# Two decode layers on one core: how the weights change places between the first layer and the second

## The chip, the cores and the metric

The kernel runs on one core of a Trainium2 chip. The metric is the device time of one execution in microseconds (us). Everything is f32. The inputs lie in HBM, and SyncE's DMA queue brings them into SBUF; the other engines compute from there.

## The reference

Two layers are computed, each an attention over a cache and then a GELU block, with the same weights and the same caches both times:

```python
x = A_x
x = x + _A_ref(_layernorm(x), A_k_cache, A_v_cache, A_wq, A_wo)
x = x + _B_ref(_layernorm(x), B_w1, B_b1, B_w2, B_b2)
x = x + _A_ref(_layernorm(x), A_k_cache, A_v_cache, A_wq, A_wo)
x = x + _B_ref(_layernorm(x), B_w1, B_b1, B_w2, B_b2)
# _A_ref: q = x @ wq (32 heads of 128), scores against k (4 key heads, 4096 long),
#         softmax, p @ v, then @ wo
# _B_ref: gelu(x @ w1 + b1) @ w2 + b2
```

There are B = 8 sequences with one token each, D = 1024, F = 3584. wq and wo have 16 MiB each, w1 and w2 14 MiB each, and k and v 64 MiB each. Read twice each, that is 376 MiB; what stays in SBUF between the layers needn't be read again.

## The kernel before

SBUF holds an `arena` of 52 units. A unit is 1024 columns of 128 partitions, 512 KiB. Every transfer goes through a list written out by hand, `stream`: each entry has a key, a number of units, its source and the units at which it may begin. `pump` (L207) issues entries from the head of the list as long as their units are free; `release` (L219) frees a used slot and calls `pump`. SyncE thus issues the DMAs in the list's order, each when the last readers of its units have ended, and nothing overtakes. Units 48 to 51 (`OWN`) are the kernel's own, for the softmax rows and their transposes.

For a sequence b, `attention` (L434) goes through eight pieces of K, each 1 MiB (`scores`, L341: 4 matmuls of 512 columns), then `probs` and `turn` (maximum, exponential, transposes), then eight pieces of V (`values`, L393), with `heads` after each pair. Layer 0 goes through the sequences 0 to 7, layer 1 through 7 to 0, so that the K of sequence 7 is kept. In layer 0 the caches pass through units 16 to 47, 16 units (8 MiB) at a time. Units 0 to 15 hold half of wq throughout; a further part of wq is parked in PSUM (`spot`) and in `spare`.

`expand` (L233) multiplies the normalized rows xnT with wq or w1; `project` (L317) multiplies with wo or w2. After wo and after w2, `layernorm` (L178) needs the whole row x before anything of wq or w1 can begin. At the turn of the layers the program ends w2, norms x and then goes through wq: half of it is resident, seven transfers bring the rest. 15 of the 28 row tiles of w2 stay for layer 1 (7.5 MiB), all eight pieces of sequence 7's K too. In layer 1 the 13 other tiles of w2 come last; the tiles that were kept are multiplied while w1's second half arrives (`begin`, L555). `add_b2` (L323) adds the bias by matmuls into the same sums.

A matmul of the program stands as two instructions in the profile.

Of the kernel before, what the change touches and what calls it, by code (L numbers as in the profile page):

```python
# [8 lines left out]
F32 = mybir.dt.float32  # L9
# [27 lines left out]
OWN = 48  # L37
RING = 32
R_AT = (48, 50)
CACHE_AT = (16, 48), (0, 32)  # L40
CUTS = {(0, "k", B - 1): (4, 2, 2), (0, "v", B - 1): (2, 2, 2, 2), (1, "v", B - 1): (4, 4), (1, "k", B - 2): (4, 4), (1, "v", 0): (4, 4)}
# [6 lines left out]
class Arena:  # L48


    def __init__(self, ap):
        self.ap = ap
        self.freed = dict.fromkeys(range(N_UNIT), 0)
        self.clock = 0
        self.limit = OWN

# [9 lines left out]
    def own(self):  # L66
        return self.take(1, range(OWN, N_UNIT))

# [29 lines left out]
def decode_layers(ctx: ExitStack, tc: tile.TileContext, x, kc, vc, wq, wo, w1, w2, out):  # L98
# [29 lines left out]
    oxT = const.tile([P, HQ * B + NT * B + PAD], F32, name="oxT")  # L128
# [9 lines left out]
    nc.gpsimd.memset(oxT[:, HQ * B:], 0.0)  # L138
    nc.gpsimd.memset(qz, 0.0)
# [38 lines left out]
    def layernorm(xr, rsum):  # L178
        pt = small_ps("pt")
        for i in range(2):  # L180
# [3 lines left out]
            xnT[:, 0:NT * B].rearrange("p (j i b) -> p j i b", j=4, i=2),  # L184
# [48 lines left out]
    def expand(name, unit, rs, finish, hooks={}, last=None):  # L233
        for u in range(2):
            acc = ps_o.tile([P, CH], F32, tag="o", name="acc")
            at = 0
            begun = set()
            end = NT * unit
            starts = [P * sum((unit // P - e + 3) // 4 for e in range(j)) for j in range(5)]
            for i, slot in enumerate(tiles((name, u))):  # L240
                c = 0
                while c < slot.cols and at < end:
                    kt, a = divmod(at, unit)
                    n = min(unit - a, slot.cols - c)
                    for j in range(4):
                        d0, d1 = max(a, starts[j]), min(a + n, starts[j + 1])
                        if d0 < d1:
                            nc.tensor.matmul(acc[32 * j:32 * j + 32, d0 - starts[j]:d1 - starts[j]],  # L248
                                             xnT[:, kt * B:kt * B + 32], slot.ap[:, c + d0 - a:c + d1 - a],
                                             start=(j not in begun), stop=(kt == NT - 1 and d1 == starts[j + 1]))  # L250
                            begun.add(j)
                    c += n
                    at += n
                if last and u == 1 and at == end:
                    last(slot.ap)
# [5 lines left out]
            row = row_s  # L261
            full = unit // CH * P
            nc.vector.tensor_scalar(row[:, 0:full], acc[:, 0:full], rs, None, op0=ALU.mult)
            if unit % CH:
                h = 32 * (unit % CH // P)
                nc.vector.tensor_scalar(row[0:h, full:], acc[0:h, full:], rs[0:h], None, op0=ALU.mult)
            pending.append(lambda u=u, row=row: finish(u, row))

    def turned(row, nt):
        pt = small_ps("pt")  # L270
        for i in range((nt + 3) // 4):
            h = 32 * min(4, nt - 4 * i)
            nc.tensor.transpose(pt[:, i * P:i * P + h], row[0:h, i * P:(i + 1) * P], ident[0:h, 0:h])  # L273
        return pt[:, 0:nt * 32].rearrange("p (t q) -> p t q", q=32)[:, :, 0:B]

    def query_unit(u, row):
        src = turned(row, 2 * REP)
        for e in range(2):
            c = Q_AT[2 * u + e]
            at = c // QW * QW  # L280
            nc.vector.tensor_copy(qz[:, at:at + B * QW].rearrange("p (b c) -> p c b", b=B)[:, c - at:c - at + REP], src[:, e * REP:(e + 1) * REP])

    def hidden_unit(u, row):
        nt = NFT // 2
        t0 = u * nt
        src = turned(row, nt)
# [10 lines left out]
        if u == 1 and st["layer"] == 0:  # L297
            nc.gpsimd.memset(qz[:, 0:2 * nt * B], 0.0)

    def products(y, name, ks, lhs, n, i0, m, hooks={}):  # L300
        for i, slot in zip(range(m), tiles(name, i0)):
            for c in range(0, slot.cols, D):
                kt = ks[n]
                for j in range(4):
                    nc.tensor.matmul(y[32 * j:32 * j + 32, 0:Q4], lhs[:, kt * B:kt * B + 32],  # L305
                                     slot.ap[:, c + j * Q4:c + (j + 1) * Q4],
                                     start=(n == 0), stop=(n == len(ks) - 1))
                n += 1
                if n in hooks:
                    hooks[n](y)  # L310
                if n == NR:
                    flush()
            release(slot)
            flush()
        return n

    def project(name, ks, lhs, out_row, resid, rsum, hooks={}, begun=None):  # L317
        y, n, i = begun or (ps_o.tile([P, CH], F32, tag="o", name="y"), 0, 0)
        n = products(y, name, ks, lhs, n, i, len(ks), hooks)
        assert n == len(ks)  # L320
        nc.vector.scalar_tensor_tensor(out_row, y[:, 0:Q4], 1.0, resid, op0=ALU.mult, op1=ALU.add, accum_out=rsum)  # L321

    def add_b2(y):  # L323

# [296 lines left out]
```

## Time and profile before

| | |
|---|---|
| time, median of 3 runs | 868.6 us (868.52 to 868.63) |
| profiled execution, its own time | 868.32 us |
| its span in the profile | 866.4 us |
| read from HBM | 367.74 MB |
| granted TensorE clock, mean | 0.796 |
| TensorE busy | 531.6 us (61%) |
| VectorE busy | 182.7 us (21%) |
| ScalarE busy | 49.0 us (6%) |
| SyncE's queue q1, share of 16 engines | 98.8% |

The profile is one execution. Its line of busy tenths has 40 slices of 21.66 us. Busy times of different engines overlap, so they are not to be added up; where an engine waits, a row names what released it. "PEld" is the loading of a matmul's stationary operand. A row of the windows view gives one stretch of the span, with the rate in GB/s last.

### The profile page before, as it was taken

Reading aid. Unit: us, or ns where it says so; the run is one execution under the profiler, and the core shown is the slowest. Engines: PE = TensorE matmul, PEld = TensorE weight load, DVE = VectorE, ACT = ScalarE, POOL = GpSimd, SP = SyncE. Lnnn points to the kernel's source line nnn. Section 1 sums busy time; section 2 is a strip of 40 time slices with the busy share of each in tenths; the row PEclk is TensorE's granted clock in tenths of the full one; section 3 lists DMA queues with packets and bytes.
Section 4 is the critical chain, followed back from the end, with each engine's and each line's share of the span. In section 5 each row is a group of like instructions: output and inputs, shape, how many; then the busy total and the mean of one; then the engine's idle time right before and its main releaser. Section 6 shows DMA issues by size and latency. Waiting matters only on the chain.

```text
span 866.4 us, 8938 instructions
## 1 busy us (share of the span) xinstructions
PE 531.6 (61%) x3998; PEld 189.2 (22%) x3998; DVE 182.7 (21%) x588; ACT 49.0 (6%) x76; POOL 1.7 (0%) x11
## 2 busy tenths in 40 slices
PE   0557665645657556756649764665756557675586
PEld 0212121211212122223223211121212112122233
DVE  0012232313122223200201231222323131231011
ACT  0010000000000000000001100000000000000010
POOL 0000000000000000000000000000000000000000
PEclk9967787777777879878879986787787777777799
DMA  9999999999999999999999999999999999999996
GB/s 393 437 436 433 433 433 433 436 430 433 436 434 433 436 406 425 433 430 428 428 422 381 431 452 433 430 433 430 436 421 436 433 430 436 417 444 433 415 426 281
DMA packets 12135, 368.44 MB, mean 425 GB/s; under 512 B 1345, under 2 KB 1601, under 8 KB 2753
## 3 DMA queue, kind: packets, MB, share of 16 engines
q1 hardware_dynamic: 11952, 367.73, 98.8%
q8 instruction: 31, 0.51, 0.2%
q10 hardware_dynamic: 144, 0.15, 0.0%
q14 instruction: 8, 0.06, 0.0%
HBM read 367.74 MB, written 0.13 MB: 425 GB/s over the span
## 4 chain that ended last, share of the span: by engine, by line
DMA 71%; PE 24%; DVE 2%; another core or an unknown queue 1%; issue 1%; ACT 0%; SPq 0%; ACTq 0%; DVEq 0%
DMA arena<-in_k_dram 46%; PE sps L350 16%; DMA arena<-in_w_dram 12%; DMA arena<-in_wo_dram 7%; DMA arena<-in_wq_dram 6%; PE acc L248 3%; PE y L305 2%; PE o_ps L400 2%; DVE arena L355 1%; PE sps L381 0%; DVE scr L405 0%; ACT arena L371 0%; PE sps L273 0%; PE sps L412 0%
## 5 line engine op out<-in xcount | busy, mean ns | idle before, releaser
L350 PE MATMUL sps<-arena,qz 128*32 128x512 f32 x1024 | 147.3, 721 | 108.0 <-DMA arena<-in_k_dram 95.5
L400 PE MATMUL o_ps<-arena 128*32 128x512 f32 x1024 | 158.0, 747 | 15.4 <-DMA arena<-in_v_dram 15.3
L305 PE MATMUL y<-arena,oxT 128*32 128x256 f32 x960 | 74.3, 468 | 51.4 <-DMA arena<-in_wo_dram 35.1
L248 PE MATMUL acc<-arena,oxT 128*32 128x512 f32 (+3 forms) x518 | 70.2, 641 | 22.7 <-DMA arena<-in_w_dram 12.5
L350 PEld LDWEIGHTS sps<-arena,qz 128*32 128x32 f32 x1024 | 35.1, 129 | 216.3 <-issue 103.1
L405 DVE SCALAR_TENSOR_TENSOR scr<-o_ps,bits,scr 128x128 f32<-128x128 f32 x192 | 67.3, 351 | 6.8
L355 DVE TENSOR_SCALAR_CACHE_REDUCE arena<-sps 128x512 f32<-128x512 f32 x32 | 22.1, 692 | 209.0 <-PE sps L350 209.0
L305 PEld LDWEIGHTS y<-arena,oxT 128*32 128x32 f32 x960 | 36.4, 132 | 87.1 <-issue 35.0
L381 PE MATMUL sps<-ident,arena 128*128 128x128 f32 x128 | 31.0, 388 | 37.5 <-DVE oxT L413 22.7
L400 PEld LDWEIGHTS o_ps<-arena 128*32 128x32 f32 x1024 | 31.4, 129 | 79.4 <-issue 60.2
L371 ACT ACTIVATE arena<-arena,bits 128x1024 f32<-128x1024 f32 x16 | 18.4, 1147 | 535.2 <-DVE scr L368 535.2
L412 PE MATMUL sps<-bits,scr 128*128 128x8 f32 x128 | 25.9, 274 | 35.0 <-DVE scr L405 29.4
L403 DVE TENSOR_SCALAR scr<-o_ps,bits 128x128 f32<-128x128 f32 x64 | 22.5, 351 | 108.7 <-PE o_ps L400 108.7
L412 PEld LDWEIGHTS sps<-bits,scr 128*128 128x128 f32 x128 | 20.0, 197 | 89.8 <-DVE scr L405 80.2
L248 PEld LDWEIGHTS acc<-arena,oxT 128*32 128x32 f32 x518 | 22.9, 123 | 60.0 <-issue 30.9
L381 PEld LDWEIGHTS sps<-ident,arena 128*128 128x128 f32 x128 | 19.8, 191 | 44.0 <-ACT arena L371 27.8
L364 PE MATMUL sps<-scr,bits 128*128 128x128 f32 x32 | 7.8, 326 | 21.3 <-DVE scr L360 21.3
L387 DVE COPY arena<-sps 128x512 f32<-128x512 f32 x16 | 11.1, 692 | 44.2 <-PE sps L381 44.2
L321 DVE SCALAR_TENSOR_TENSOR xb<-y,xb 128x256 f32<-128x256 f32 x4 | 1.7, 424 | 85.1 <-PE y L305 85.1
L413 DVE TENSOR_TENSOR oxT<-sps,scr 128x8 f32<-128x8 f32 x64 | 11.0, 171 | 40.1 <-PE sps L412 40.1
L181 PE MATMUL sps<-ident,xb 128*128 128x128 f32 x16 | 4.0, 338 | 25.1 <-DMA xb<-in_x_dram 23.4
L389 PE MATMUL sps<-scr,bits 128*128 128x32 f32 x32 | 10.2, 412 | 12.5 <-DVE arena L387 12.5
(67 smaller groups left out, 130.4 us busy)
## 6 DMA issues: line engine op xcount, KB each, us to landing
arena<-in_w_dram SPq DMA_DIRECT2D x9, 3072.0 KB, 20.1
arena<-in_v_dram SPq DMA_DIRECT2D x4, 4096.0 KB, 20.4
arena<-in_k_dram SPq DMA_DIRECT2D x3, 4096.0 KB, 24.9
arena<-in_wo_dram SPq DMA_DIRECT2D x4, 3072.0 KB, 18.8
arena<-in_v_dram SPq DMA_DIRECT2D x4, 2048.0 KB, 23.6
arena<-in_w_dram SPq DMA_DIRECT2D x4, 2048.0 KB, 22.1
arena<-in_wq_dram SPq DMA_DIRECT2D x5, 1024.0 KB, 9.1
arena<-in_k_dram SPq DMA_DIRECT2D x2, 2048.0 KB, 28.6
```

The costliest lines, as they stand in the source:

```text
L248: nc.tensor.matmul(acc[32 * j:32 * j + 32, d0 - starts[j]:d1 - starts[j]], xnT[:, kt * B:kt * B + 32], slot.ap[:, c + d0 - a:c + d1 - a], ...
L305: nc.tensor.matmul(y[32 * j:32 * j + 32, 0:Q4], lhs[:, kt * B:kt * B + 32], slot.ap[:, c + j * Q4:c + (j + 1) * Q4], start=(n == 0), stop= ...
L350: nc.tensor.matmul(ps[32 * g:32 * g + 32, :], qz[:, c:c + 32], kt[:, g * CH:(g + 1) * CH], start=(j == 0), stop=(j == HKV - 1))
L355: nc.vector.tensor_scalar(st["row", b].ap[:, half * CH:(half + 1) * CH], ps, SCALE, None, op0=ALU.mult, op1=ALU.max, accum_out=st["mx", b] ...
L371: nc.scalar.activation(row, row, AF.Exp, bias=bias, scale=1.0, accum_out=ls)
L381: nc.tensor.transpose(pp[:, t * P:(t + 1) * P], row[:, c:c + P], ident)
L387: nc.vector.tensor_copy(dst, src)
L400: nc.tensor.matmul(o[32 * g:32 * g + 32, :], s[:, g], v[:, g * CH:(g + 1) * CH], start=(half == 0), stop=(half == NH - 1))
L403: nc.vector.tensor_scalar(r, o[:, 0:P], sel_t[:, 0:1], None, op0=ALU.mult)
L405: nc.vector.scalar_tensor_tensor(r, o[:, t * P:(t + 1) * P], sel_t[:, t:t + 1], r, op0=ALU.mult, op1=ALU.add)
L412: nc.tensor.matmul(po[:, 0:REP], r_s[j % 2], sel_h, start=True, stop=True)
L413: nc.vector.tensor_tensor(oT_v[:, j * REP:(j + 1) * REP, b], po[:, 0:REP], rl_s[b % 2][:, j * REP:(j + 1) * REP], ALU.mult)
```

## The change

The turn of the layers is written anew, as `swap`. w2 is now laid out in four column blocks of D (`_blocks`), 7 units each: 4 row tiles of a block are a unit of their own (key w2u), the other 24 are 4 + 2 units. The queries of layer 1 no longer wait for the norm: xnT gets the plain x of a block as soon as that block of w2 is summed, 256 entries of D, and the two row tiles of wq that belong to them are multiplied (`q_part`), used up and freed. Mean and scale are applied to the queries behind it: a ninth column of ones in xnT (`XS`) gives the column sums of wq, and `moments` gives mean and scale. The next blocks of w2 are loaded into the freed units of wq.

So all of wq stays in layer 0 (28 units, and the last row tile parked), and all of w2 but 4 of 28 row tiles stays for layer 1. Of sequence 7's K six pieces stay. For that, the caches pass through 20 units (28 to 47) in layer 0, in transfers of 4 to 8 units, and through 24 in two areas in layer 1, in transfers of 4 to 12. wo, w1 and the last V pieces of layer 0 go through three blocks of 4 units (`BLOCK_AT`). w1 is split into hidden parts of 2048, 1024 and 512 (`GROUPS`) instead of two halves, so GELU runs three times per layer. b2 is added to x by `bias_row`, after w1's first transfer.

```diff
-OWN = 48
-RING = 32
-R_AT = (48, 50)
-CACHE_AT = (16, 48), (0, 32)
+OWN = range(48, 52), (6, 7, 14, 15)
+LAST_BLOCKS = 32, 48, 28
+AREAS = ((28, 48),), ((16, 28), (36, 48))
+BLOCK_AT = 28, 32, 48
+XS = B + 1
+CB = D // Q4
+UK = 4
+GROUPS = 2048, 1024, 512
...
+    def bias_row():
+        y = small_ps("s")
         for h in range(2):
             dg = scr[:, 0:CH]
             nc.vector.tensor_tensor(
...
+                nc.tensor.matmul(y[32 * j:32 * j + 32, 0:Q4], ones[:, 0:32], dg[:, j % 2 * Q4:(j % 2 + 1) * Q4], start=True, stop=True)
+        nc.vector.tensor_tensor(x_row, x_row, y[:, 0:Q4], ALU.add)
...
+    def down(y, c, kts, j=None):
+        for kt in kts:
+            g = kt % 4 if j is None else j
...
+            nc.tensor.matmul(y[32 * g:32 * g + 32], hT[:, kt * B:kt * B + 32], w2_at[c, kt], ...)
...
+    def swap():
...
+        def transient(c):
+            slot = arrive(("w2u0", c), c, 0)
+            down(half(c), c, range(UK))
+            release(slot)
+        ys = small_ps("s")
+        transient(0)
+        flush()
...
+        for c in range(CB):
+            for e, k0 in enumerate((UK, UK + 16)):
+                arrive(("w2", c, e), c, k0)
+            down(half(c), c, range(UK, NFT))
+            ysb = row_s[:, c % 2 * Q4:(c % 2 + 1) * Q4]
+            nc.vector.tensor_copy(ysb, half(c))
+            if c + 1 < CB:
+                transient(c + 1)
+            for i in range(2):
+                nc.tensor.matmul(pt[:, i * B:(i + 1) * B], ysb[:, i * P:(i + 1) * P], bsel, start=True, stop=True)
+            xc = xv[:, 2 * c:2 * c + 2]
+            nc.vector.tensor_tensor(xc, pt[:, 0:2 * B].rearrange("p (i b) -> p i b", b=B), xc, ALU.add)
+            nc.tensor.matmul(pt[32 * c:32 * c + 32, Q4:2 * Q4], sel_x, ysb, start=True, stop=True)
...
+            for kt in (2 * c, 2 * c + 1):
+                for u in range(2):
+                    if kt < NT - 1:
+                        slot = held.pop(("q", kt, u))
+                        q_part(acc, u, kt, 0, slot.ap)
+                        release(slot)
...
-    weights(("q0", 0), wq[0], [16], fixed(0), kept=lambda i: [(("q1", 0), e) for e in range(8)])
-    weights(("q0", 1), wq[1], [16], fixed(RING))
-    stream.extend(caches(0, orders[0], ()))
...
-    weights("p1", w2[0], [6, 4, 1, 1, 1], fixed(16, 24, 28, 22, 23), early * D, 6)
+    weights(("q0",), wq[0], [16, 8, 4, 4], fixed(0, 16, 24, 28), kept=halves)
+    ring = around(AREAS[0], 4, 8)
...
+    i, j, k = LAST_BLOCKS
+    add(down_weights(0, ("u", 0, 1), 0), i + 3, j, i)
+    add(down_weights(1, ("u", 0, 1), 0), i + 2, k, i + 2)
+    add(down_weights(2, (0, 1, "u"), 0), 0, 4, 6)
+    add(down_weights(3, ("u", 0, 1), 0), 7, 8, 12)
+    stream.append((("qe", 0), 1, wq[0][:, -W:-KEEP], (6,), ()))
+    stream.extend(cache(1, last_b, "k", listed((4, (16,))), n_kept))
+    stream.extend(cache(1, last_b, "v", listed((4, (20,)), (4, (24,)), (4, (36,)), (4, (40,)))))
+    ring = around(AREAS[1], 20, 12)
...
+    weights(("o1",), wo[0], [8, 12, 12], fixed(20, 36, 16))
+    for u, (sizes, spots) in enumerate((([12, 4], (36, 16)), ([4, 4], (20, 24)), ([2, 1, 1], (36, 38, 39)))):
+        weights(("i1", u), w1[0][:, at:at + NT * GROUPS[u]], sizes, fixed(*spots))
...
+    for c in range(CB):
+        add(down_weights(c, ("u",), 1), 40 + c)
```

How this moves the instructions is seen at three places. First TensorE (PE) at the turn of the layers, before the change: L305 is w2, L331 the bias, L181, L182 and L176 layernorm, L248 wq, L273 the transposes of the queries, L350 the scores.

```order
L305 MATMUL y<-arena,oxT 32x256 x32
L331 MATMUL y<-scr,bits 32x256 x4
L305 MATMUL y<-arena,oxT 32x256 x80
L181 MATMUL sps<-ident,xb 128x128
L182 MATMUL sps<-bits 128x128
L181 MATMUL sps<-ident,xb 128x128
L182 MATMUL sps<-bits 128x128
L176 MATMUL sps<-bits 32x1 x4
L248 MATMUL acc<-arena,oxT 32x512 x4
```

The same place after it: L371 is w2, L407 and L410 bring a block's sums into xnT and into x, L292 is wq.

```order
L371 MATMUL sps<-arena,oxT 32x256 x28
L407 MATMUL sps<-bits,scr 128x8 x2
L410 MATMUL sps<-scr,bits 32x256
L292 MATMUL acc<-arena,oxT 32x512 x16
L371 MATMUL sps<-arena,oxT 32x256 x28
L407 MATMUL sps<-bits,scr 128x8 x2
L410 MATMUL sps<-scr,bits 32x256
L292 MATMUL acc<-arena,oxT 32x512 x16
```

w2 and wq now alternate, and the last 4 of each 28 products of w2 are the next block's first ones, `transient(c + 1)`; they stand ahead of the 16 products with wq, which are two of its row tiles.

Second, SyncE's DMAs at the same turn, before the change, from the last of w2 (in_w) over wq to the caches of layer 1:

```order
L214 DMA arena<-in_w_dram 128x3072 x2
L214 DMA arena<-in_w_dram 128x1024 x3
L214 DMA arena<-in_wq_dram 128x1024
L214 DMA arena<-in_wq_dram 128x2048 x5
L214 DMA arena<-in_wq_dram 128x1152
L214 DMA arena<-in_v_dram 128x8192 x2
L214 DMA arena<-in_k_dram 128x8192 x2
```

And after it, from block 1's second piece of w2 on:

```order
L221 DMA arena<-in_w_dram 128x2048
L221 DMA arena<-in_w_dram 128x4096
L221 DMA arena<-in_w_dram 128x2048
L221 DMA arena<-in_w_dram 128x1024 x2
L221 DMA arena<-in_w_dram 128x4096
L221 DMA arena<-in_w_dram 128x2048
L221 DMA arena<-in_wq_dram 128x128
L221 DMA arena<-in_k_dram 128x4096
L221 DMA arena<-in_v_dram 128x4096 x4
L221 DMA arena<-in_k_dram 128x4096
L221 DMA arena<-in_k_dram 128x12288
```

Of wq one piece of 128 columns is left. Blocks 2 and 3 of w2 stand between the rest of w2 and the caches, and their units are those that wq gives up. The 128x12288 is the first transfer of 12 units in layer 1.

Third, TensorE at the end of layer 1 after the change: L254 is w1, L183 and L361 variance and bias, L275 and L273 the turn of a hidden part ahead of its GELU, L371 w2. The row ahead of these is layernorm.

```order
L254 MATMUL acc<-arena,oxT 32x512 x24
L183 MATMUL sps<-bits 32x1 x4
L361 MATMUL sps<-scr,bits 32x256 x4
L254 MATMUL acc<-arena,oxT 32x512 x8
L254 MATMUL acc<-arena,oxT 32x256 x16
L275 MATMUL sps<-ident,scr 128x128 x4
L371 MATMUL y<-arena,oxT 32x256 x48
L254 MATMUL acc<-arena,oxT 32x256 x16
L254 MATMUL acc<-arena,oxT 32x512 x4
L275 MATMUL sps<-ident,scr 128x128 x2
L254 MATMUL acc<-arena,oxT 32x512 x4
L273 MATMUL sps<-bits,scr 128x8 x4
```

Behind these stand 64 more products with w2, then the program ends. Before the change the last 60 products of w2 stood behind the second of two GELU parts.

More of the change, by code (lines that the diff above doesn't have):

```diff
@@ new lines, in lane, with cache @@
+    def lane(layer, b, a, r, m):
+        where = k_at if a == "k" else v_at
+        keys = [(a, *where(b, e)) for e in range(r, r + m)]
+        for e, key in enumerate(keys):
+            pieces[layer, key] = ((layer, keys[0]), e)
+        return (layer, keys[0]), (kc if a == "k" else vc)[b][:, r * W:(r + m) * W]
+    def cache(layer, b, a, at, r=0):
+        while r < NR:
+            n, starts = at(2 * (NR - r))
+            name, src = lane(layer, b, a, r, n // 2)
+            yield (name, n, src, starts, ())
+            r += n // 2
@@ L505, in decode_layers, with listed @@
+    def listed(*spots):
+        spots = iter(spots)
+        return lambda left: next(spots)
     rsum = row_sums()
     nc.vector.tensor_reduce(rsum, x_row, AX.X, ALU.add)
-    kept = {("k", *k_at(B - 1, r)) for r in range(NR)}
+    last_b = B - 1
+    n_kept = 6
+    kept = {("k", *k_at(last_b, r)) for r in range(n_kept)}
     orders = [list(range(B)), list(range(B))[::-1]]
-    early = NFT // 2 + 1
-    first_ks = [6, 7, 8, *range(6), *range(9, early)]
+    any_of = lambda *at: lambda k, i: at
@@ L534, in decode_layers @@
+    queries(rs)
     for layer in range(2):
         st["layer"] = layer
+        last = attention(orders[layer], kept if layer == 0 else (), {("turn", last_b): opened} if layer == 0 else {})
+        rsum = row_sums()
+        project(f"o{layer}", oT, x_row, rsum, {4: last})
         rs = layernorm(x_row, rsum)
         if layer == 0:
-            expand("q0", W, rs, query_unit, last=park)
-        else:
-            held["q1", 1, "end"] = Kept(spare)
-            expand("q1", W, rs, query_unit, {(1, 1): lambda: unpark((("q1", 1), len(last_q)))})
```

350 lines of the change are left out of this document (235 added, 115 removed).

## The prediction

> **What bounds the kernel now.** First the page: the busy line of the DMA engines, the queues, and the chain that ended last by engine.
>
> ```profile
> span 866.4 us, 8938 instructions
> DMA  9999999999999999999999999999999999999996
> q1 hardware_dynamic: 11952, 367.73, 98.8%
> DMA 71%; PE 24%; DVE 2%; another core or an unknown queue 1%; issue 1%; ACT 0%; SPq 0%; ACTq 0%; DVEq 0%
> ```
>
> SyncE's queue (q1) keeps the 16 DMA engines busy for 98.8% of the span. So the time is bytes over rate, plus the moments in which that queue runs dry, plus what follows the last landing. TensorE only matters where it frees room too late. Next, the windows view, by stage. The columns are the window, its length, busy time of PE, PEld, DVE, ACT and POOL, the granted clock, the DMA share and GB/s.
>
> ```profile
> 110.00:290.00 180.00, 111.69 (x704) 35.66 (x696) 47.87 (x157) 9.19 (x15) 0.00 (x0) 0.77 1.00 431
> 352.00:400.00 48.00, 29.95 (x304) 13.01 (x297) 5.16 (x17) 0.00 (x0) 0.00 (x0) 0.79 1.01 431
> 399.60:461.00 61.40, 36.88 (x348) 17.57 (x351) 6.83 (x21) 3.93 (x7) 0.28 (x1) 0.81 1.00 424
> 455.00:476.00 21.00, 19.63 (x228) 8.35 (x232) 2.33 (x8) 2.21 (x5) 0.00 (x0) 0.90 0.94 380
> 847.00:862.00 15.00, 12.29 (x190) 6.94 (x190) 2.91 (x9) 0.30 (x1) 0.00 (x0) 1.00 0.79 330
> ```
>
> The reader sees 431 GB/s in the cache stage (8 MiB transfers) and in the wo stage (2 and 3 MiB), 424 in the w1 and w2 stage (0.5 to 3 MiB), 380 at today's turn of the layers, and 330 as the queue drains at the end. Third, SyncE's waits and its last issue.
>
> ```profile
> SPq L214 <- PE sps L176: 11.7, 1, 11.7
> 863.64 0.35 SPq L563 DMA_DIRECT2D out_dram<-xb  x1
> ```
>
> At the turn SyncE waited 11.7 us once, until layernorm released wq's next slot; that is the dip to 380.
>
> **The change, part by part.** Below, 1 MiB stands for 1.049 MB / 431 GB/s = 2.43 us.
>
> *Bytes.* Counted from the program's transfers: 367.59 MB now, 358.68 MB after. wq is no longer read twice (22.06 to 16.06 MiB), w1 and w2 go from 48.5 to 44 MiB, and K rises from 120 to 122 MiB, as six pieces instead of eight are kept. 8.91 MB / 431 GB/s = **-20.7 us**.
>
> *Smaller transfers.* 82 become 122; the 30 of 8 MiB become 2 to 6 MiB. The 352 to 400 row (2 and 3 MiB) shows no loss, the 399.6 to 461 row 1.6%. The caches' 262 MB take 608 us, so the bounds are 0 and +10; I take **+3**, nearer the first row, whose sizes these are.
>
> *Today's dip goes.* 21 us x (1 - 380/431) = **-2.5 us**.
>
> *The turn, first dry spell.* The rows for PE's pace, and for a restart after an idle queue:
>
> ```profile
> 455.63 8.39 PE L305 MATMUL y<-arena,oxT 128*32 128x256 f32 x120 [7.19 <-DMA arena<-in_w_dram]
> 459.05 4.49 PEld L305 LDWEIGHTS y<-arena,oxT 128*32 128x32 f32 x84 [0.23 <-issue]
> 301.62 3.64 PE L350 MATMUL sps<-arena,qz 128*32 128x512 f32 x32 [0.83 <-DVE arena L355]
> out_dram<-xb SPq DMA_DIRECT2D x1, 128.0 KB, 1.7
> ```
>
> After 7.19 us of idleness the first 36 products of 256 columns take 3.42 us (0.095 us each and more), the other 84 4.49 us (0.053); 512 columns take 0.114 warm, so about 0.22 cold. 128 KB need 0.3 us at 431 GB/s, so an issue into an empty queue costs 1.4 us. (Each matmul of the program is two in the profile.)
>
> Count from the end of w1's last transfer. The stream then has, in MiB: 0.5, 2, 1 (block 0 of w2), 0.5, 2, 1 (block 1), 2, 1, 0.5 (block 2), 0.5 (block 3's first), which is 11 MiB. Their slots come free in time (the nearest is block 1's last MiB, which waits for `transient(1)`, some 2 us ahead; without that cover it would be one more dry place, 2.5), so the queue runs dry at 26.8 us. Block 2's first rows, key w2u0 2, land at 25.5. Block 3's main part needs units 8 to 11, which `wq`'s tile 2 gives up, and on PE that tile stands behind `transient(2)`, which needs w2u0 2. PE has ended block 1 by about 21 and waits some 5 us, so it restarts cold: 8 products of 256 columns 0.9, the block's sums into xnT 0.6, 16 products of 512 columns 3.6, restart 1.4. First bytes at 32.0: dry for **+5.2 us**; at warm pace 3.0. The draining queue also lands its last transfers late: the 847 to 862 row lost 15 x (1 - 330/431) = 3.5 us. I take **+1.5** (0 to 3.5), as w2u0 2 is the last but one.
>
> On the pace the Trainium skill, "TensorE: Matmul & The Clock Gate", section "What's actually happening", says that the array runs at half clock after an idle window of about 3.4 us and until about 3.4 us of work are done. The 3.42 us above agree. By that page a wait under its window would leave PE warm and the spell would be 3.0.
>
> *The turn, second dry spell.* Rows for one batch's middle and its values:
>
> ```profile
> 337.58 0.69 DVE L355 TENSOR_SCALAR_CACHE_REDUCE arena<-sps 128x512 f32<-128x512 f32 x1 [4.72 <-PE sps L350]
> 345.50 4.95 PE L400 MATMUL o_ps<-arena 128*32 128x512 f32 x24
> 474.92 0.41 DVE L281 COPY qz<-sps 128x64 f32<-128x64 f32 x2 [0.82 <-PE sps L273]
> 855.84 6.25 PE L305 MATMUL y<-arena,oxT 128*32 128x256 f32 x112 [1.88 <-DVE oxT L296]
> ```
>
> From 32.0 on the stream has 2, 1 (block 3), 2 (K), four times 2 (V), 2 (next K): 15 MiB, to 68.5. The 6 MiB after these need units 16 to 27, held until the fourth V piece is used. PE: rest of tile 2 and 3 to 33; block 2 (48 x 0.056) 2.7; tiles 4 and 5 with the sums 4.8; block 3 2.7; tiles 6 and 7, the moments 5.2; copy, transposes, twelve small VectorE steps at 0.2 and the first scores from 53; four pieces 1.8, 0.8, four pieces 3.6 to 59.2; to the first values 7.9 (337.58 to 345.50) or a little less; four value pieces 6.3 (4.95 for three); restart 1.4: 74.8. Dry for 6.3; I take **+5** (3 to 6.5), since no earlier heads stand in the middle of this first batch.
>
> *The start* costs nothing: wq comes in four pieces instead of two, but 8 MiB of K are issued behind it before the first wait, which is 19.5 us of cover for the last piece's 16 products and the turn of the queries; without that cover it would be one dry place, 2.5.
>
> *Layer 0's ring* shrinks from 32 units to 20: 10 MiB, 24.3 us, of which 7.9 us per batch free nothing. Followed batch by batch, an issue comes within 2 us of the queue's end at three places (before the keys of batch 5, at the last batch's values, at wo). The price of one such place is today's 2.5, so 0 to 7.5; I take **+3.5**.
>
> *The tail.* Rows of the GELU and of the b2 addition now, and of the end:
>
> ```profile
> 838.63 0.75 PE L273 MATMUL sps<-ident,scr 128*128 128x128 f32 x4
> 842.27 0.28 DVE L296 SCALAR_TENSOR_TENSOR oxT<-qz 128x112 f32<-128x112 f32 x1 [1.45 <-ACT qz L294]
> 846.81 0.69 DVE L327 TENSOR_TENSOR scr<-ident,xb 128x512 f32<-128x512 f32 x1 [3.66 <-PE y L331]
> 847.55 0.41 PE L331 MATMUL y<-scr,bits 128*32 128x256 f32 x2 [0.78 <-DVE scr L327]
> 853.21 0.75 PE L273 MATMUL sps<-ident,scr 128*128 128x128 f32 x4 [0.29 <-DVE scr L263]
> 855.50 0.28 DVE L296 SCALAR_TENSOR_TENSOR oxT<-qz 128x112 f32<-128x112 f32 x1
> 862.48 0.64 PE L305 MATMUL y<-arena,oxT 128*32 128x256 f32 x8 [0.39 <-DMA arena<-in_w_dram]
> 863.18 0.42 DVE L321 SCALAR_TENSOR_TENSOR xb<-y,xb 128x256 f32<-128x256 f32 x1 [7.40 <-PE y L305]
> ```
>
> Now 13 units of w2 follow w1, and only 8 matmuls stand behind the last landing: 862.4 to 866.4, 4.0 us. After, only four units follow w1, so PE ends the kernel. From the landing of layer 1's first w1 transfer (6 MiB): 48 matmuls of 512 columns, cold at first, 7.2; variance and b2 (0.7 + 2 x 0.69 + 2 x 0.41) 3.1; 16 more 1.8; 32 of 256 columns 1.8; first GELU 3.9 (838.63 to 842.55); 96 products of w2 5.4; 32 more 1.8; 8 of 512 0.9; second GELU 2.2 (2.6 at 853.21, for twice the width); scale and turn of the third part 1.2; 128 products of w2 7.2. That is 36.5, and 3.2 for the addition and the output: 39.7. The stream behind that landing is 10 MiB, 24.3 us, so the end comes 15.4 after the last landing, +11.4; the 3.5 us of late last landings are no longer on the path: **+7.9**.
>
> *Sum:* 866.4 - 20.7 + 3 - 2.5 + 5.2 + 1.5 + 5 + 3.5 + 7.9 = 869.3 of span. The profiled execution takes 868.32, 1.9 over its span, and the median of the runs is 0.3 above it: **871.5 us**. With g for all dry time (15.2), the time is 856.3 + g.
>
> **The rivals.**
> *Faster.* The dry spells close: PE stays warm at the turn (3.0), nothing lands late, the second spell is 3, the ring costs nothing: g = 6 gives 862.3. It decides at g = 10.6. For it: of today's span SyncE's own queue holds 0% of the chain, so the kernel as it stands has room to spare nearly everywhere. Against it: the wait before `transient(2)` is in the order itself.
> *No change:* g between 10.6 and 14.0, and the bytes are paid back exactly, 868.6.
> *Slower by much.* Each transfer has a price of its own, and 40 more pay it. The 399.6 to 461 row holds 14 transfers and loses 1.0 us against 431, 0.07 us each: 3 us for 40, which the sum has. But a place that runs dry costs 2.5, and layer 0's caches now come in 42 transfers through a ring of 24.3 us; from the fourth dry place on it is worse than the forecast, and with five, 12.5 instead of 3.5, the time is 880. Against it: followed one by one, only three come within 2 us of the queue's end. [...]
> *It doesn't do what it says:* the program's transfers show wq read once but for 64 KiB, so this is left out.
>
> **How the numbers follow.** Forecast 0.50, faster 0.25, no change 0.13, slower by much 0.12. A run of this kernel can tell about 0.2%, 1.7 us, from no change. Faster than 866.9 is 0.25, within 0.13, slower than 870.3 0.62. The forecast's own range is 870 to 877; the range that reaches to the other cases, with the transfers' 0 to +10, is 862 to 881.
>
> **What would show it.** Right: about 358.8 MB on q1; in the windows a dip of some 6 us of DMA in the turn, while PE waits at L371 for a w2 landing; a second one before the first 6 MiB of K in layer 1; the last weight landing about 15 us before the end, with PE busy at L371. Wrong: a queue at 431 GB/s through the turn, or a last landing within 6 us of the end (then it is faster), or dips at most of layer 0's batches (then slower).

## The result: 4.2% slower

The changed kernel takes 904.4 us (median of 4 runs, 903.3 to 906.9), the kernel before 868.6 beside it (868.3 to 868.6): ratio 1.0417, 95% interval 1.0394 to 1.044. The forecast was 871.5 with a range of 862 to 881: the sign is right, the size is wrong by 33 us. The profiled execution took 903.69 us, its span 901.9.

The page of the changed kernel, the same lines as of before, with the line of rates in 40 slices of 22.55 us:

```profile
span 901.9 us, 9145 instructions
DMA  9999999999999998999996979999999999999990
GB/s 400 421 440 417 431 392 433 429 390 419 397 438 412 427 427 315 379 428 429 405 382 239 404 317 427 420 413 435 430 426 430 423 418 433 429 428 428 419 406 11
q1 hardware_dynamic: 17712, 358.82, 94.2%
DMA 48%; PE 37%; DVE 8%; ACT 3%; issue 2%; another core or an unknown queue 1%; SPq 0%; ACTq 0%; DVEq 0%
```

The queue's share falls from 98.8% to 94.2%, and the chain that ended last goes over TensorE (PE) for 37% of the span instead of 24%. The low slices lie in three places: down to 390 at several places of layer 0, 315 and 379 where its last sequence ends, 239 at the turn of the layers and 317 behind it, in layer 1's first sequence. The last slice, 11 GB/s, is the tail. The windows view by stage (window, length, busy time of PE, PEld, DVE, ACT, POOL, granted clock, DMA share, GB/s):

```profile
110.00:290.00 180.00, 115.86 (x664) 36.61 (x664) 44.74 (x146) 9.19 (x15) 0.00 (x0) 0.74 0.98 414
310.00:352.00 42.00, 27.33 (x152) 8.34 (x152) 11.08 (x41) 3.08 (x5) 0.00 (x0) 0.72 0.95 401
352.00:400.00 48.00, 29.79 (x242) 11.77 (x242) 7.47 (x24) 0.60 (x1) 0.00 (x0) 0.71 0.92 374
438.00:476.00 38.00, 22.77 (x223) 10.14 (x221) 6.34 (x24) 2.08 (x4) 0.31 (x1) 0.81 0.91 365
476.00:482.00 6.00, 5.74 (x31) 1.83 (x34) 0.17 (x1) 0.00 (x0) 0.00 (x0) 0.51 0.01 3
522.00:529.00 7.00, 6.61 (x42) 1.46 (x34) 2.65 (x9) 0.00 (x0) 0.00 (x0) 0.70 0.29 101
862.00:881.00 19.00, 13.53 (x173) 6.88 (x169) 4.24 (x11) 1.85 (x3) 0.00 (x0) 0.91 0.90 372
881.00:901.90 20.90, 15.75 (x202) 8.53 (x194) 4.00 (x15) 0.48 (x2) 0.00 (x0) 0.99 0.02 7
```

From 110 to 290 us the rate is 414 where it was 431. From 476 to 482 almost nothing moves (3 GB/s). Behind 881 there are 21 us with no weight left to load.

The packets' records of the two traces give the whole span in four parts: the start, the bytes at the rate that the 16 engines had while they worked, their idle share up to the last weight's landing, and what follows it.

| | before | after | difference |
|---|---|---|---|
| first packet | 1.7 | 1.7 | 0 |
| bytes / rate while working | 367.59 MB / 430.8 GB/s = 853.3 | 358.68 / 424.4 = 845.2 | -8.1 |
| engines idle before the last landing | 7.0 | 33.9 | +26.9 |
| behind the last landing | 4.4 | 21.1 | +16.7 |
| span | 866.4 | 901.9 | +35.5 |

At the old rate the saved bytes are worth 20.7 us, as forecast. The lower rate takes back 12.6, the dry places 26.9, the tail 16.7.

By place, the engines stand idle longer than before by 10.7 us in layer 0 (70 to 400 us), by 8.9 at the turn (438 to 505) and by 6.9 in layer 1's first sequence (505 to 535).

### The profile page after: what moved, and what is told of

The parts are those of the page before. It is cut to its first block, busy times and chain, and to the rows that moved or that the text cites. A ratio compares the mean times of both kernels' runs of the same rounds, so it can differ in the third digit from the quotient of the medians.

```text
span 901.9 us, 9145 instructions
## 1 busy us (share of the span) xinstructions
PE 556.9 (62%) x4034; PEld 193.9 (22%) x4034; DVE 189.5 (21%) x616; ACT 50.1 (6%) x78; POOL 1.9 (0%) x12
## 3 DMA queue, kind: packets, MB, share of 16 engines
q1 hardware_dynamic: 17712, 358.82, 94.2%
## 4 chain that ended last, share of the span: by engine, by line
DMA 48%; PE 37%; DVE 8%; ACT 3%; issue 2%; another core or an unknown queue 1%; SPq 0%; ACTq 0%; DVEq 0%
DMA arena<-in_k_dram 25%; PE sps L488 13%; PE o_ps L538 8%; DMA arena<-in_w_dram 7%; DMA arena<-in_wo_dram 6%; DMA arena<-in_v_dram 5%; DMA arena<-in_wq_dram 5%; PE sps L519 3%; PE acc L254 2%; ACT arena L509 2%; DVE arena L493 2%; PE y L371 2%; PE y L341 2%; PE acc L292 2%; PE sps L371 1%
## 5 line engine op out<-in xcount | busy, mean ns | idle before, releaser
L488 PE MATMUL sps<-arena,qz 128*32 128x512 f32 x1024 | 167.2, 805 | 118.1 <-DMA arena<-in_k_dram 109.5
L538 PE MATMUL o_ps<-arena 128*32 128x512 f32 x1024 | 162.5, 762 | 11.1 <-DMA arena<-in_v_dram 11.1
L488 PEld LDWEIGHTS sps<-arena,qz 128*32 128x32 f32 x1024 | 38.9, 139 | 242.1 <-issue 130.2
L341 PE MATMUL y<-arena,oxT 128*32 128x256 f32 x512 | 40.9, 481 | 39.8 <-DMA arena<-in_wo_dram 39.8
L538 PEld LDWEIGHTS o_ps<-arena 128*32 128x32 f32 x1024 | 31.4, 131 | 78.0 <-issue 62.4
L254 PE MATMUL acc<-arena,oxT 128*32 128x512 f32 (+1 forms) x288 | 34.7, 616 | 17.0 <-DMA arena<-in_w_dram 16.4
L292 PE MATMUL acc<-arena,oxT 128*32 128x512 f32 (+1 forms) x250 | 34.4, 662 | 4.6 <-DMA arena<-in_wq_dram 4.3
L341 PEld LDWEIGHTS y<-arena,oxT 128*32 128x32 f32 x512 | 18.7, 134 | 61.6 <-DMA arena<-in_wo_dram 39.1
L371 PE MATMUL sps<-arena,oxT 128*32 128x256 f32 x224 | 17.8, 444 | 9.8 <-DMA arena<-in_w_dram 8.7
L254 PEld LDWEIGHTS acc<-arena,oxT 128*32 128x32 f32 x288 | 11.0, 127 | 36.1 <-issue 18.9
## 6 DMA issues: line engine op xcount, KB each, us to landing
arena<-in_k_dram SPq DMA_DIRECT2D x16, 2048.0 KB, 16.7
arena<-in_wo_dram SPq DMA_DIRECT2D x8, 2048.0 KB, 11.5
```

What stands on the lines that cost most here:

```text
L254: nc.tensor.matmul(out_j, xnT[:, kt * XS:kt * XS + 32], src, start=(j not in begun), stop=(kt >= NT - (4 if split else 1)))
L292: nc.tensor.matmul(acc[u][32 * j:32 * j + 32, d0 - j * CH:d1 - j * CH], xnT[:, kt * XS:kt * XS + 32], ap[:, d0 - c0:d1 - c0], start=(kt == ...
L341: nc.tensor.matmul(y[32 * j:32 * j + 32, 0:Q4], lhs[:, n * B:n * B + 32], slot.ap[:, c + j * Q4:c + (j + 1) * Q4], start=(n == 0), stop=(n ...
L371: nc.tensor.matmul(y[32 * g:32 * g + 32], hT[:, kt * B:kt * B + 32], w2_at[c, kt], start=first, stop=(kt >= NFT - 4 if j is None else kt = ...
L488: nc.tensor.matmul(ps[32 * g:32 * g + 32, :], qz[:, c:c + 32], kt[:, g * CH:(g + 1) * CH], start=(j == 0), stop=(j == HKV - 1))
L538: nc.tensor.matmul(o[32 * g:32 * g + 32, :], s[:, g], v[:, g * CH:(g + 1) * CH], start=(half == 0), stop=(half == NH - 1))
```

## The experiments

"Faster by" below is the difference of the ratios to the kernel before, times 868.5 us; the changed kernel stands at 1.0417. The intervals of these ratios reach 0.1 to 0.3% to each side, 1 to 3 us. A "product" or a "row" of TensorE's work below is one matmul instruction of the profile, two of which make a matmul of the program. A landing is the end of a transfer's last packet. Theory: room in the arena comes free too late, at places set by TensorE's order and pace, and at the end TensorE itself is late. Rival: smaller transfers cost by themselves.

**Size alone.** The kernel before, ring of 32 units kept:

```diff
-                for m in CUTS.get((layer, a, b), (NR,)):
+                for m in CUTS.get((layer, a, b), (2, 2, 2, 2)):
```

> The kernel before, its ring of 32 units unchanged, but nearly all K and V transfers of both layers cut to 4 units (2 MiB) in place of 16 units (8 MiB). Theory 'ring' (the changed kernel loses its time in layer 0 because 20 units free too late, not because transfers are small): within 4 us of the kernel before, 868 to 873. Rival 'size' (small transfers go at a lower rate: 421 GB/s at 16 KB a partition in the trace after, against 432 at 64 KB before, over some 600 us of caches): 8 to 15 us slower, 877 to 884, and the stretch from 110 to 290 us runs at 421 to 426 GB/s instead of 431.

873.8 us, 1.0067 (1.0052 to 1.0082), +5.8 us; between the two. Its window:

```profile
110.00:290.00 180.00, 114.07 (x696) 36.20 (x699) 46.51 (x149) 7.95 (x13) 0.00 (x0) 0.78 1.01 428
```

The queue is never dry (1.01), and the rate is 428 for 431. Over all its bytes it has 427.9. So size costs about 6 us where nearly all K and V transfers are of 2 MiB, not 3, and not 33.

**Ring alone.** The kernel before with only the caches of sequences 0 to 6 moved, once through 20 units, once through 32, in transfers of up to 8 units (the function `around` is the changed kernel's):

```diff
+                if layer == 0 and b < B - 1:
+                    while r < NR:
+                        n, at = ring(2 * (NR - r))
...
-    weights(("q0", 1), wq[1], [16], fixed(RING))
+    weights(("q0", 1), wq[1], [16], fixed(16))
+    ring = around(((28, 48),), 4, 8)
```

> The kernel before, with the K and V of layer 0's sequences 0 to 6 sent through units 28 to 47 alone, in the changed kernel's sizes (4 to 8 units); nothing else of the change. Theory 'ring': the queue runs dry at most changes of sequence, 10 to 15 us slower, 879 to 884, with SyncE waiting for the last V pieces. Rival 'size': the same as the run with 32 units and the same sizes, both 2 to 6 us slower. My own blind term for this ring was 3.5 us (0 to 7.5), less the last sequence and wo, which stay as before here.

> As the run with 20 units, but with the ring left at 32 units (16 to 47) and the transfers of sequences 0 to 6 at 8 units (4 MiB). Theory 'ring': within 2 us of the kernel before, 867 to 871. Rival 'size': 2 to 6 us slower, like the run with 20 units.

With 32 units 868.2 us, 1.0008 (0.9999 to 1.0018); with 20 units 881.9, 1.0151 (1.0121 to 1.0182), +13.1 us. That is the ring's theory, but part of it was my own doing. The rows of the two runs, 20 units first:

```profile
190.00:230.00 40.00, 25.05 (x146) 7.92 (x146) 9.64 (x31) 1.37 (x3) 0.00 (x0) 0.75 0.94 400
352.00:400.00 48.00, 27.05 (x234) 10.12 (x233) 6.67 (x21) 0.00 (x0) 0.00 (x0) 0.70 0.87 365
```

```profile
190.00:230.00 40.00, 26.48 (x154) 8.47 (x153) 9.83 (x32) 2.44 (x4) 0.00 (x0) 0.76 1.00 431
352.00:400.00 48.00, 30.29 (x308) 13.28 (x304) 5.53 (x18) 0.00 (x0) 0.00 (x0) 0.79 1.00 427
```

In the 365 row wo's first transfer stood behind the last V piece, because the last V pieces had taken their units in another order. So the run was made again with these in order, and once more with transfers of 4 units only:

```diff
-                        at = range(lo, hi, 2 * m)
+                        at = (lo + 2 * r,) if layer == 0 else range(lo, hi, 2 * m)
...
-    ring = around(((28, 48),), 4, 8)
+    ring = around(((28, 48),), 4, 4)      # second run only
```

> The first run with 20 units again (the kernel before, layer 0's sequences 0 to 6 through units 28 to 47 in transfers of 4 to 8 units), with the last V pieces in the order of their units: in the first run wo stood behind the last of them, and 365 GB/s in the stretch from 352 to 400 us (48 us, some 7 us lost) came from that and not from the ring. So this run is the price of the ring for seven sequences alone. Theory 'ring by sequence': 6 to 8 us slower than the kernel before, 874 to 877. My blind term for the ring, 3.5, would be 869 to 872 with what lies outside these sequences taken off.

> The same with transfers of 4 units only. Theory 'late slot' (a transfer of 8 units lands as a whole, TensorE then has four pieces of K to go through at half clock before the softmax, and the next slot comes free only at the fourth V piece, 20.3 us after the landing in the trace after at 180.97, with 20.7 us of stream left): room comes a piece or two earlier on both sides, no dry place is left, 1 to 3 us slower than the kernel before (the lower rate of 2 MiB transfers), 869 to 871. Rival 'depth' (20 units are too few in any cut): as the run with 4 to 8 units or slower, 875 to 880.

875.6 us, 1.0086 (1.0069 to 1.0103), +7.5; and 871.3, 1.0038 (1.0023 to 1.0053), +3.3. The windows, first the run with up to 8 units, then with 4:

```profile
190.00:230.00 40.00, 24.97 (x146) 8.01 (x146) 9.82 (x32) 1.84 (x3) 0.00 (x0) 0.74 0.94 399
230.00:270.00 40.00, 25.57 (x148) 8.22 (x148) 9.03 (x30) 1.84 (x3) 0.00 (x0) 0.74 0.97 411
```

```profile
190.00:230.00 40.00, 25.52 (x152) 8.04 (x152) 10.49 (x33) 2.32 (x4) 0.00 (x0) 0.76 1.00 427
230.00:270.00 40.00, 25.22 (x148) 7.53 (x148) 9.17 (x32) 1.84 (x3) 0.00 (x0) 0.80 1.01 427
```

Cut by 4, the ring of 20 doesn't run dry. It is not the depth, it is the size of a slot against what TensorE does behind a landing. The timeline of the changed kernel shows it at sequence 3 (L488 `scores`, L538 `values`):

```profile
182.78 6.35 PE L488 MATMUL sps<-arena,qz 128*32 128x512 f32 x32 [3.67 <-DMA arena<-in_k_dram]
197.58 4.92 PE L538 MATMUL o_ps<-arena 128*32 128x512 f32 x24
```

The last 4 MiB of K landed at 182.19. TensorE began 0.59 us later, took 6.35 us for four pieces, mostly at half clock (granted 0.57), and reached the first V at 197.58. The next K transfer, 8 units, begins in the units of that last K transfer and ends in those of the first two V pieces, so it stood behind the softmax and was issued at 201.29, 19.1 us after the landing. (The expectation above counts from 180.97, where the last packet began, and speaks of the fourth V piece; it is the second.) Behind the landing lay 8 MiB of V, which ended at 201.69, 19.5 us after it; the issue's first packet came at 202.26. In transfers of 4 units the first K of a sequence needs only the last K of the sequence before, and goes ahead of the softmax.

**The same in the changed kernel.**

```diff
-    ring = around(AREAS[0], 4, 8)
+    ring = around(AREAS[0], 4, 4)
```

> The changed kernel, its 20 units of layer 0 used in transfers of 4 units only, none of 8. If the ring of 20 is short because an 8-unit slot comes free only when its fourth piece is used, room comes 2 pieces earlier: 6 to 10 us faster than the changed kernel, 894 to 898. If it is short by its depth alone: within 2 us of it, 902 to 906. Rival 'size': 3 to 5 us slower, 907 to 909.

902.3 us, 1.0401 (1.0373 to 1.0428): 1.4 us faster, which the intervals don't tell from no change and which is what "depth" had expected. But the trace does not read so. First the page's rates in this run, then a row of its tail in the timeline, then the same row of the changed kernel:

```profile
GB/s 400 421 427 429 423 428 430 428 428 425 429 427 428 427 427 306 391 429 428 411 297 360 344 384 426 443 358 438 430 429 427 403 412 432 450 408 429 421 334 7
```

```profile
871.61 7.07 PE L371 MATMUL y<-arena,oxT 128*32 128x256 f32 x96 [3.39 <-DVE oxT L331]
```

```profile
876.44 5.39 PE L371 MATMUL y<-arena,oxT 128*32 128x256 f32 x96 [3.39 <-DVE oxT L331]
```

The low slices of layer 0 are gone (421 to 430), and the first w1 transfer of layer 1 landed 4.2 us earlier (851.88 for 856.04). Then TensorE gave 2.7 us back at the end: as in this row, products ran at half clock in this run (granted 0.50 from 872.22 to 875.63) that ran at full clock in the other. Of layer 0's dry places only the last sequence's (306, 391) is left.

**The turn, first spell.**

```diff
-            if c + 1 < CB:
-                transient(c + 1)
+            if c == 0:
+                transient(1)
...
+            if 0 < c < CB - 1:
+                transient(c + 1)      # behind the row tiles of wq
```

> The changed kernel with the first four row tiles of blocks 2 and 3 (transient) multiplied behind the two row tiles of wq instead of ahead of them; the stream is the same. In the trace after, TensorE stands idle for 7.47 us before it, and the queue is empty from 474.84 to 482.05 us. Theory 'order' (the wait for w2u0 2 ahead of wq's tile 2 makes this spell): the spell goes and all behind it moves up, 6 to 8 us faster than the changed kernel. Rival 'shifted' (the next slot is late anyway, since the later tiles depend on the same landings): 0 to 2 us faster, with a spell of the same size a few us later.

899.1 us, 1.0347 (1.0332 to 1.0363): 6.1 us faster. The changed kernel's timeline at this place (L371 w2, L292 wq), and then the window of 438 to 482 with the order altered:

```profile
474.24 1.08 PE L371 MATMUL sps<-arena,oxT 128*32 128x256 f32 x8 [7.47 <-DMA arena<-in_w_dram]
477.40 5.80 PE L292 MATMUL acc<-arena,oxT 128*32 128x512 f32 x29
```

```profile
438.00:476.00 38.00, 28.20 (x299) 12.19 (x295) 6.93 (x23) 3.57 (x6) 0.31 (x1) 0.91 0.98 395
476.00:482.00 6.00, 5.90 (x81) 2.63 (x73) 0.04 (x1) 0.00 (x0) 0.00 (x0) 1.00 0.83 304
```

The wait of 7.47 us for w2u0 2 was the cause: the 6 us with 3 GB/s are gone, and the clock there is 1.00 for 0.51.

**The turn, second spell.**

```diff
-    ring = around(AREAS[1], 20, 12)
+    ring = around(AREAS[1], 20, 4)      # the next sequence's K only
```

> The changed kernel with the 12 units of layer 1's second K (units 16 to 27) loaded by three transfers of 4 units instead of one. Theory 'slot' (the second dry spell, 522.88 to 528.78 us, is the wait of one 12-unit transfer for three slots, the last of which comes free at the fourth V piece): 4 to 6 us faster than the changed kernel. Rival 'TensorE late': the first 4 units go at once, but the ones behind wait for the same V pieces, 1 to 2 us faster.

898.2 us, 1.0342 (1.0321 to 1.0363): 6.5 us faster, theory 'slot'. Its window over the place:

```profile
510.00:530.00 20.00, 13.37 (x82) 5.03 (x85) 6.51 (x21) 3.12 (x4) 0.00 (x0) 0.74 1.01 421
```

**The tail.**

```diff
-    (([12, 4], (36, 16)), ...
+    (([4, 4, 4, 4], (36, 40, 44, 16)), ...
```

> The changed kernel with layer 1's first w1 transfer of 12 units cut into three of 4, in the same units. Theory 'TensorE ends the kernel' (end 21 us after the last landing; 48 rows of products wait for 6 MiB): these rows move ahead of the last landings, and the chain behind starts from the next w1 transfers instead, 4 to 7 us faster than the changed kernel, with the last landing where it was. Rival 'the queue ends it': no change within 1 us.

900.1 us, 1.0359 (1.0344 to 1.0375): 5.0 us faster. What lies behind the last landing falls from 21.1 to 19.3 us, and that landing comes at 878.8 for 880.8. So TensorE ends the kernel, as the theory had it, but of the 3.8 us between these two executions only 1.8 lie behind the last landing. The theory had left that landing where it was; of the other 2.0, 1.8 arose ahead of the edited place (layer 1's second norm began at 848.59 for 850.40), and why is open.

**All of these together**, and the last products of w2 in another order:

```diff
             for c in range(CB):
                 arrive(("w2u1", c), c, 0)
-                down(y[0], c, range(UK), c)
+            for kt in range(UK):
+                for c in range(CB):
+                    down(y[0], c, [kt], c)
```

> The changed kernel with the late transient, the cut first w1 transfer, the cut second K and the layer-0 transfers of 4 units together, and the last four row tiles' products (w2u1) taken by row tile and then by block instead of by block and then by row tile. In the trace after, these 32 rows take 0.112 us each, where those that change the block each time take 0.054: 1.8 us. If the places add up (7 + 5 + 5 + 2 + 2): 21 us faster than the changed kernel, 883. If a place that is mended uncovers the next: 8 to 14 us faster, 890 to 896. Slower than the kernel before either way, since the ring of 20 units and the tail remain.

886.0 us, 1.0189 (1.016 to 1.0219): 19.8 us faster. The four single gains make 19.0, and the turned loops were expected to give some 2 more, so within the intervals they add up. Then layer 1's ring too:

```diff
-    ring = around(AREAS[1], 12, 12)
+    ring = around(AREAS[1], 12, 4)
```

> The run with all mends, and in layer 1 too K and V in transfers of at most 4 units instead of 12. In its trace the queue still runs dry before the 12-unit K transfers at 583, 628, 672 and 703 us, about 6 us together. Theory 'late slot': 4 to 6 us faster than the run with all mends, 880 to 882. Rival 'depth': within 2 us of it, 884 to 888. Slower than the kernel before either way: the last batch of layer 0, the smaller transfers and the 20 us behind the last landing remain.

878.4 us, 1.0131 (1.0104 to 1.0158): another 5.0 us, theory 'late slot'. The windows from 500 to 800 us, before this edit and behind it:

```profile
500.00:800.00 300.00, 185.96 (x1182) 59.89 (x1182) 76.40 (x247) 15.27 (x25) 0.00 (x0) 0.77 0.99 420
```

```profile
500.00:800.00 300.00, 189.54 (x1182) 60.48 (x1182) 76.46 (x249) 15.98 (x25) 0.00 (x0) 0.80 1.01 428
```

**GELU early.** In `expand`:

```diff
             pending.append(lambda ...: finish(u, row, split))
+            if st["layer"] == 1 and u == 0:
+                flush()
```

> The run with all mends and 4-unit transfers in both layers, and in layer 1 the GELU of the first hidden part as soon as its sums are whole, instead of after the first transfer of the next part. In that run's trace TensorE has the sums of the first part at 842.3 us, turns them at 848.64 behind 32 other rows, stands idle for 3.40 us for the GELU, and takes 6.65 us for the 96 rows of w2 behind it; the last landing is at 859.6 and the end at 876.7. Theory 'chain' (TensorE's order alone sets the end): the GELU runs under the wait for the next landing, 3 to 5 us faster, 873.5 to 875.5. Rival 'clock' (work moved earlier runs at half clock, or the last landing takes over): within 1.5 us of it, 877 to 880.

870.4 us, 1.003 (1.0019 to 1.0042): 8.8 us faster, more than the theory 'chain' had. The timeline of its tail (L277 turns the sums, L254 w1, L373 w2) and the window behind its last landing:

```profile
840.09 0.66 PE L277 MATMUL sps<-ident,scr 128*128 128x128 f32 x4 [0.85 <-DVE scr L264]
841.81 3.08 PE L254 MATMUL acc<-arena,oxT 128*32 128x256 f32 x32 [1.06 <-DMA arena<-in_w_dram]
844.64 5.97 PE L373 MATMUL y<-arena,oxT 128*32 128x256 f32 x96
857.65 7.11 PE L373 MATMUL y<-arena,oxT 128*32 128x256 f32 x128
```

```profile
856.30:867.90 11.60, 8.10 (x136) 5.03 (x136) 1.87 (x8) 0.23 (x1) 0.00 (x0) 1.00 0.04 13
```

The idle 3.40 us ahead of the 96 rows is gone, and 11.6 us are left behind the last landing for 17.0 in the run before it: 5.4 us are the edit's. Another 3.0 are not: layer 1's second norm began at 825.54 for 828.54, ahead of the place that the edit touches. Half of them lie where layer 0's last sequence ends (392 GB/s from 310 to 352 us for 377).

**Size once more**, with the dry places mended: layer 1 in transfers of up to 8 units, then layer 0 of up to 6 as well.

```diff
-    ring = around(AREAS[1], 12, 4)
+    ring = around(AREAS[1], 12, 8)
...
-    ring = around(AREAS[0], 4, 4)
+    ring = around(AREAS[0], 4, 6)      # second run only
```

> The last run (all mends, 4-unit transfers, GELU early) with layer 1's K and V in transfers of up to 8 units. Theory 'rate' (a 2 MiB transfer runs at 426 GB/s and a 4 MiB one at 430 in the traces so far, and with PE's order mended the ring of 24 units has room for 8): some 300 us at 0.9%, 2 to 3 us faster, 867.5 to 868.5. Theory 'late slot' (a slot of 8 comes free too late in any order): dry places come back, 1 to 4 us slower, 871 to 875.

> The same, and layer 0's ring of 20 units in transfers of up to 6 units (3 MiB, 428.5 GB/s where 2 MiB had 426). Theory 'rate': 1 to 1.5 us faster than with 4, 866 to 867.5, faster than the kernel before by a little. Theory 'late slot': with three pieces to a slot the queue runs dry again at some of the sequences, as it did with 4 to 8 units, 2 to 5 us slower than with 4, 870 to 873.

871.1 us, 1.0037 (1.0024 to 1.0049), and 872.0, 1.0046 (1.0033 to 1.006). Both times lie where "late slot" had put them, but its mechanism is not there, and "rate" has the mechanism without the time. The rate does rise; the same window with transfers of 4 units and of up to 8:

```profile
500.00:800.00 300.00, 196.99 (x1182) 61.98 (x1182) 76.43 (x247) 13.71 (x24) 0.00 (x0) 0.74 1.01 428
```

```profile
500.00:800.00 300.00, 198.73 (x1182) 63.12 (x1182) 76.43 (x247) 15.66 (x25) 0.00 (x0) 0.75 1.01 431
```

These are 2.1 us, and no dry place came back there. But the total is not lower than with 4 units, and the intervals overlap. In the profiled executions the 2 us go at a place that the edit doesn't touch, the last sequence of layer 0; with 4 units first, then with 8:

```profile
310.00:352.00 42.00, 27.91 (x166) 8.65 (x170) 10.68 (x34) 1.84 (x3) 0.00 (x0) 0.74 0.94 392
```

```profile
310.00:352.00 42.00, 28.83 (x154) 8.74 (x158) 10.19 (x33) 1.84 (x3) 0.00 (x0) 0.66 0.90 373
```

That is 1.9 us, with a lower granted clock (0.66 for 0.74). These two executions lie at the fast end of the one kernel's runs and the slow end of the other's, so the pair doesn't settle the medians.

No version here beats the kernel before; the nearest is 0.3% slower. The four parts of that run's span (4-unit transfers, GELU early) are 1.7 + 358.68 MB / 425.4 GB/s (843.1) + 11.5 idle + 11.6 behind the last landing = 867.9 us. So of the 20.7 us that the bytes save, the rate takes 10.5, the dry places 4.5 and the tail 7.2. Of the idle 11.5, 5.1 lie from 310 to 400 us, where layer 0's last sequence ends; no run here mends that place.

## Why the prediction was wrong, by its own steps

Its sum was 869.3 of span against 901.9, 32.6 short: 9.6 in the rate, 17.7 in the dry places (with the late last landings, which the table counts there) and 5.3 in the tail. Of the 17.7, 7.2 are layer 0's, 4.7 the turn's, 1.9 the second spell's and 2.7 the late last landings', which are late here too.

- *Bytes*, -20.7: right (358.82 MB on q1).
- *Smaller transfers*, +3 of 0 to 10: mis-sized. Size alone is 5.8 us (first run). In the changed kernel the rate costs 12.6. Mending most of the dry places (11.5 us idle for 33.9 in the run with GELU early) brought back only some 2 of it, so restarts there are not the other half. About 5 of the 10.5 that are left are the caches' smaller transfers, as in the first run; the rest lies mainly at the places that still run low, and its cause is open.
- *The first dry spell*, +5.2: right in place and cause (6.1 by the run that takes it away). Its cover failed: I had block 1's last MiB "some 2 us ahead" and priced its loss at 2.5 us. In the trace it was issued at 459.38, as the queue was running out: 203 GB/s from 458.5 to 461 us, 0.9 us of idle engines. Block 2's first transfer, issued at 462.55, left another 0.2. With these, low rates and the start of the spell it is 365 GB/s from 438 to 476. The timeline there (L254 w1, L371 w2):

```profile
440.70 3.53 PE L254 MATMUL acc<-arena,oxT 128*32 128x256 f32 x32 [2.38 <-DMA arena<-in_w_dram]
452.83 5.30 PE L371 MATMUL sps<-arena,oxT 128*32 128x256 f32 x48 [1.26 <-DMA arena<-in_w_dram]
```

  Both at half clock (0.110 us a row): the first holds the slot of block 0's main part, which was issued at 444.27 only, the second is block 0, and such a block I had at 2.7.
- *The second spell*, +5: right (6.5).
- *Today's dip goes*, -2.5: its place is taken by these.
- *Layer 0's ring*, +3.5 of 0 to 7.5: the step that failed. Idle engines alone cost 10.7 us there. With the lower rate it is 7.5 us in seven sequences alone (3.7 of them idle engines), and about 8.5 in the last sequence and wo (from the 401 and 374 rows, against the 427 of the run with 32 units: 42 x 0.061 + 48 x 0.124). Elsewhere in the sum I had TensorE's four pieces of K at 3.6 us right behind a landing; they take 6.35, and start 0.59 after it. Those 3.3 us are more than the 2 us of margin that I read as "near". So the rival "dips at most of layer 0's batches" was the truer one, by slots and not by a price for each DMA.
- *The tail*, +7.9: right in kind, mis-sized. The chain from the landing of the first w1 transfer to the end was 39.7 by my count (the 3.1 for variance and b2 come to 2.9 by their rows) and is 45.9. Three parts make 5.4 of the 6.2 us: the start after the landing, the rows at half clock, the rows of w2u1. The timeline:

```profile
856.58 7.38 PE L254 MATMUL acc<-arena,oxT 128*32 128x512 f32 x48 [4.85 <-DMA arena<-in_w_dram]
867.15 5.31 PE L254 MATMUL acc<-arena,oxT 128*32 128x512 f32 x46
888.87 9.77 PE L371 MATMUL y<-arena,oxT 128*32 128x256 f32 x128
```

The landing is at 856.04, the start 0.54 later. The rows at 867.15, with 0.6 for two more, I had at 1.8 + 1.8. The 128 last ones I had at 7.2; they take 9.77, and 7.11 in the run with GELU early, which has them in the altered order.

What held all of this up was the belief that "TensorE only matters where it frees room too late", with its durations taken mostly warm. After the change it frees room too late at each of the three places above, and at the end it is late itself.

## What to carry to other kernels

When a ring gets smaller, write down for one round the time from the landing of a slot to the moment that the slot it lets in is issued, with the start after the landing and with the engine at its slow pace, and compare it with what is still queued: here 19.1 us against 19.5 was already dry, as an issue takes another 0.96 us to its first packet. If it is short, cut the slots before giving the ring more room; four units instead of eight brought 4.2 us of 7.5 back in the kernel before. And an order that saves bytes at one place has to be paid at each place where the last reader of a slot waits for something else, so look at what stands ahead of it on its engine.

## What the runs showed of the hardware

- From the end of a transfer's last packet to the first product that waits for it: 0.59 us (K, 182.19 to 182.78) and 0.54 us (w1, 856.04 to 856.58). From an issue into an empty queue to its first packet: 0.96 us. Together 1.5, close to the 1.4 that I had taken for a restart. The Trainium skill, "DMA: Bandwidth & Descriptors", section "Anatomy of one DMA", puts most of about 2.0 us fixed behind the last byte, but for DMAs that GpSimd issues. No run here uses that path, and on SyncE's queue the part behind the last packet is 0.5 to 0.6 us.
- The same products at the same place ran at two paces: after 3.39 us of idleness 96 rows took 5.39 us in one run and 7.07 in another. In both traces the granted clock is 1.00 or 0.50 and changes only on a grid of 3.41 us steps. In the slow one the step from 868.81 to 872.22 us held 2.80 us of the idle time, and the next was granted 0.50. In the other the idle time fell into two steps, 1.31 and 2.08 us, and the clock stayed at 1.00. The Trainium skill, "TensorE: Matmul & The Clock Gate", section "What's actually happening", says that a window of about 3.4 us decides and that it is free-running; the traces agree. So the length of a wait alone doesn't tell the pace: 2.98 us of idleness were followed by 32 rows in 3.28 us (all mends together), 2.97 by 32 rows in 1.93 (the tail's run).
- The changed kernel's four runs spread over 3.6 us; the sets of 7 to 13 runs of the kernel before spread over 1.4 to 2.5. That the two paces make the difference is likely but not shown.
- Products into the same 32 output rows one after the other took 0.112 us each (by their starts, 893.42 to 895.21), those that go round the four groups of 32 rows 0.054, at full clock both. With the two loops turned, the last 128 rows took 7.11 us for 9.77; no run turns the loops alone.
